# The queries' matrix of a decode kernel: one load of 64 KB pieces in place of two of 32 KB

## The chip, the cores and the metric

The kernel runs on one core of a Trainium2 chip. Its time is the device time of one execution, in microseconds. The core has five engines that run side by side and wait for each other by semaphores: TensorE (PE in the profile), VectorE (DVE), ScalarE (ACT), GpSimd (POOL) and SyncE (SP). Transfers between the chip's memory and the on-chip buffer of 128 partitions are issued by an engine's queue and carried out by 16 DMA engines. Before the change, three runs gave 684.35 us in the median (683.91 to 684.98).

## The reference, cut to what matters

One token x of 512 numbers is normalized; xn goes into attention over a cache of 8192 keys and values for each of 32 heads of width 128, and into a gated unit; the result is x + s * g, all in 32-bit floats.

```python
xn = _layernorm(x)                                   # 512
q = (xn @ wq).reshape(32 heads, 128)                 # wq: 512 x 4096, 8.39 MB
scores = einsum("hd,hkd->hk", q, k_cache) * 128**-0.5   # k_cache: 32 x 8192 x 128, 134 MB
p = softmax(scores)
o = einsum("hk,hkd->hd", p, v_cache)                 # v_cache: 134 MB
s = o.reshape(4096) @ wo                             # wo: 4096 x 512, 8.39 MB
g = silu((sigmoid(xn @ w_gate) * (xn @ w_up)) @ w_down)   # three of 2.82 MB
out = x + s * g
```

Each weight and each cached number is used once, so 293.67 MB are read for one token.

## The kernel before, in words

The work goes through three large buffers (`slots`) of 64 KB on each of the 128 partitions. Slots 0 and 1 hold keys in turn, slot 2 holds values. A load of keys or values covers one pair of heads: 2 x 8192 rows of 128 numbers, 8.39 MB, which fills a slot with one piece of 64 KB on each partition. There are 16 pairs.

Nearly all loads are issued by SyncE, in program order, on one queue (q1 in the profile). SyncE waits in front of a load until the slot is free, and every load behind it in the program waits with it. The order is: the queries' matrix, w_gate and w_up (both in slot 0), keys of pair 0 (slot 1), w_down (slot 2, when the queries are made), keys of pair 1 (slot 0, when TensorE has summed the gate's rows), values of pair 0 (slot 2, when the gated unit is done), and then in turn the keys of pair i (when the scores of pair i-2 are done with the slot, `summed[i - 2]`) and the values of pair i-1 (when TensorE is done with the values before, `valued`). At the end the last keys and values are cut into parts, and wo comes in seven loads. All loads pass through `load` (line 168) or `load_values` (line 227).

The queries' matrix `wq` lies in slot 2 until w_down and the values need it. Partition p holds rows 4p to 4p+3 of the matrix, one after the other; so the four blocks `wq_t[:, k, :]` of 4096 numbers lie side by side on each partition, and x is turned so that `xn[:, k]` fits them. Two loads bring blocks 0 and 1, then blocks 2 and 3: 32 KB on each partition each. The first load is issued ahead of `tc.close()` and `tc.compile()`, the second behind them. ScalarE issues the two small loads of x on its own queue (q10), which the same 16 DMA engines serve.

VectorE makes the queries' products in place. When x has landed it is turned (L261) and normalized in a chain of short steps with TensorE and ScalarE (L262 to L280). Then VectorE multiplies block 0 by `xn[:, 0]` (L290), and adds blocks 1 and 2 to it (L291), 4096 numbers wide; block 3 follows in eight stretches of 512 (L308). After each stretch TensorE sums the 128 partitions by a product with ones, into a PSUM bank, and ScalarE copies the sums to `q_all` (L312). So every partition has all queries that it needs.

w_gate and w_up are taken in the same way (L290 and L291, 1376 wide), summed by TensorE, made into the hidden row (L348 to L362) and multiplied by w_down. Then VectorE turns to the pairs: for each it multiplies the keys by the queries in place (L416), and sums each row (L417), which frees the keys' slot. TensorE, ScalarE and VectorE make the softmax without its division (L409, L429, L431), and TensorE multiplies the values (64 products of 512 columns) while VectorE is at the next pair's keys. The tail divides, places the result (L466 to L476) and multiplies by wo (L521, L523).

The profile's line L38 is the helper through which all of TensorE's instructions pass.

Of the kernel before, what the change touches and what calls it, by code (L numbers as in the profile page):

```python
# [51 lines left out]
def kernel(  # L52
# [16 lines left out]
    KT = D // P  # L69
# [23 lines left out]
    W_DVE = [r for r in range(W_FOLD) if r not in [r for r, _ in W_PE]]  # L93
    V_CUT, K_CUTS = NB // 2, {NP - 2: (NB * 3 // 4,), NP - 1: (NB * 23 // 32,)}

    N_SEMS = 36
    DVE, ACT, SP, POOL = nc.vector, nc.scalar, nc.sync, nc.gpsimd
    PE = Later(nc.tensor)
    pe_only = OrderedEngineSet([nc.tensor.engine])
# [2 lines left out]

    sems = [nc.alloc_semaphore(f"s_{i}") for i in range(N_SEMS)]
    s_out = nc.alloc_semaphore("s_out")
# [42 lines left out]
    def semaphore(name):  # L147
        return unused.pop(0)
# [14 lines left out]
    def load(eng, name, dst, src, *after):  # L163
        wait(eng, *after)
        if name not in loads:
            loads[name] = [semaphore(f"s_{name}"), 0]
        loads[name][1] += 16
        ins = eng.dma_start(dst, src)  # L168
        if not tc.compiled:
            tc.no_tile_sem_insts.add(ins.ins.name)  # L170
        ins.then_inc(loads[name][0], 16)
        return loads[name][0], loads[name][1]

    def wait(eng, *steps):
        for s in steps:
            if s is not None:
                eng.wait_ge(*s)
# [9 lines left out]

    xv = x.rearrange("a b d -> (a b d)")
    wq_t = slots[2].rearrange("p (k c) -> p k c", k=KT)
    wq_v = wq.rearrange("(p k) c -> p k c", k=KT)  # L190
    def load_queries(n):
        return load(SP, f"wq{n}", wq_t[:, n:n + 2, :], wq_v[:, n:n + 2, :])

    ld_wq = [load_queries(0)]
    tc.close()
    tc.compile()
    ld_wq.append(load_queries(2))
    wg_t, wu_t = (slots[0][:, n * KT * F:(n + 1) * KT * F].rearrange("p (k f) -> p k f", f=F) for n in range(2))
    ld_g = load(SP, "wg", wg_t, w_gate.rearrange("(p k) f -> p k f", k=KT))
    ld_u = load(SP, "wu", wu_t, w_up.rearrange("(p k) f -> p k f", k=KT))  # L200
# [61 lines left out]
    t = dve(DVE.reduce_sum(st[:, 0:1], x_col, axis=AX.X))  # L262
    wait(PE, t)
    t = pe(PE.matmul(pt[:, 0:1], ones, st[:, 0:1], start=True, stop=True))
    wait(DVE, t)
    t = dve(DVE.tensor_scalar(st[:, 1:2], pt[:, 0:1], 1.0 / D, None, op0=ALU.mult))
    wait(DVE, t)
    t = dve(DVE.tensor_scalar(xc, x_col, st[:, 1:2], None, op0=ALU.subtract))
    wait(DVE, t)
    t = dve(DVE.tensor_mul(sq, xc, xc))  # L270
    wait(DVE, t)
    t = dve(DVE.reduce_sum(st[:, 2:3], sq, axis=AX.X))
    wait(PE, t)
    t = pe(PE.matmul(pm[:, 0:1], ones, st[:, 2:3], start=True, stop=True))
    wait(ACT, t)
    t = act(ACT.activation(st[:, 3:4], pm[:, 0:1], AF.Sqrt, bias=eps_t, scale=1.0 / D))
    wait(DVE, t)
    t = dve(DVE.reciprocal(st[:, 4:5], st[:, 3:4]))
# [8 lines left out]
    def in_place(w, k, cols=slice(None)):  # L287
        y = w[:, 0, cols]
        if k == 0:
            return dve(DVE.tensor_scalar(y, y, xn[:, 0:1], None, op0=ALU.mult))  # L290
        return dve(DVE.scalar_tensor_tensor(y, w[:, k, cols], xn[:, k:k + 1], y, op0=ALU.mult, op1=ALU.add))  # L291
# [1 line left out]

    wait(DVE, c_xn)
    for k in range(KT - 1):
        wait(DVE, ld_wq[k // 2] if k % 2 == 0 else None, t if k else None)
        t = in_place(wq_t, k)
    wait(DVE, t)
    before_q = PE.take()
# [5 lines left out]
    for t in range(NQ):  # L305
        c = slice(t * QT, (t + 1) * QT)
# [29 lines left out]
    for dst, src, ld in zip(sums, (wg_t, wu_t), (ld_g, ld_u)):  # L336
        wait(DVE, ld)
        for k in range(KT):
            t = in_place(src, k)
# [7 lines left out]
    for d, c in zip(sums[0], chunks):  # L347
        t = act(ACT.activation(sg[:, c], d[:, :c.stop - c.start], AF.Sigmoid))  # L348
    wait(DVE, t, rows[1])
    for d, c in zip(sums[1], chunks):  # L350
        t = dve(DVE.tensor_mul(hg[:, c], sg[:, c], d[:, :c.stop - c.start]))
# [6 lines left out]
    n = FL // NG  # L358
    for g in range(NG):
        r = slice(g * GP, (g + 1) * GP)  # L360
        h = hg[r, NG * FW + g * n:NG * FW + (g + 1) * n].rearrange("p (i c) -> p c i", c=FC)
        t = dve(DVE.transpose(hid[r, FP:, :].rearrange("p c (i m) -> p c i m", m=NG),  # L362
                              h.unsqueeze(3).to_broadcast([GP, FC, n // FC, NG])))
# [128 lines left out]
    def copies(g):  # L492
        return GP if g % 2 == 0 else 1
# [21 lines left out]
    for k, r in enumerate(W_DVE):  # L515
        n = k % 2
# [21 lines left out]
    for r in direct:  # L538
        landed(PE, r, direct)
        for g in range(NG):  # L540
            n = copies(g)
# [6 lines left out]
    t = dve(DVE.tensor_mul(g_row, g_row, acc))  # L548
# [66 lines left out]
```

## Time and profile before

| what | value |
|---|---|
| median of three runs | 684.35 us (683.91 to 684.98) |
| the profiled execution | 683.9 us |
| its span, first to last instruction | 682.5 us |
| read from memory | 293.67 MB, 430 GB/s over the span |
| SyncE's queue q1 | 6968 packets, 99.5% of 16 DMA engines' span |
| VectorE | 613.4 us busy, 90% of the span |
| TensorE | 220.8 us busy, 32% of the span, mean granted clock 0.670 |
| the two loads of the queries' matrix | 4096 KB each, 16.3 us from issue to landing in the median |

Times in rows of the profile are microseconds from the start of the span, unless marked ns. A row of the timeline has the start, the duration, the engine (a trailing q marks its queue, where DMAs are issued), the line, the operation, what is written and read, the shapes, the count, and in brackets how long the engine had been idle and what ended that. A row of a stretch has its bounds and length, the busy time of each engine with the count of its instructions, TensorE's granted clock, the mean busy share of the 16 DMA engines, and GB/s; a packet counts in the stretch in which it starts, so short stretches swing. A row of a queue has packets, MB and the time of its packets as a share of the 16 engines' time.

### The profile page before, as it was taken

The page shows a single profiled execution, that of the slowest core. Times are in us where ns is not written, and L with a number is a line of the kernel's source. Part 1 is how long each engine was busy: PE and PEld are TensorE (multiplying, and loading weights), DVE is VectorE, ACT ScalarE, POOL GpSimd, SP SyncE. Part 2 cuts the span into 40 slices and gives each one's busy share as a digit, 9 for nine tenths or more (in the row PEclk, how much of TensorE's full clock was granted, in tenths as well). Part 3 has the DMA queues.
Part 4 walks back from the last instruction along what each step waited for, and adds up shares of the span by engine and source line. Part 5 has one row for each costly group of instructions (what it writes and reads, how often), then busy time and mean ns, then how long its engine had stood idle before and what let it go on. Part 6 is the DMA issues. An engine that isn't in the chain of part 4 may idle for free. (4 is left out here: it accounts for less than half of the span.)

```text
span 682.5 us, 3396 instructions
## 1 busy us (share of the span) xinstructions
PE 220.8 (32%) x1386; PEld 63.9 (9%) x1386; DVE 613.4 (90%) x151; ACT 44.6 (7%) x142; POOL 2.6 (0%) x11
## 2 busy tenths in 40 slices
PE   0353024060513305060512306050412406053368
PEld 0120001010100101010100101010100101011111
DVE  2979999999999998998979899898989899999926
ACT  2130010000000100000000100000010100000010
POOL 0000000000000000000000000000000000000000
PEclk9985658575665758575665758575665858575869
DMA  9999999999999999999999999999999999999998
GB/s 380 430 442 461 442 430 430 430 430 430 430 430 430 430 430 430 438 446 446 453 430 430 430 430 430 430 430 430 430 430 430 430 447 422 475 422 409 436 428 341
DMA packets 6988, 293.68 MB, mean 430 GB/s; under 512 B 798, under 2 KB 812, under 8 KB 1228
## 3 DMA queue, kind: packets, MB, share of 16 engines
q1 hardware_dynamic: 6968, 293.67, 99.5%
q10 hardware_dynamic: 20, 0.01, 0.0%
HBM read 293.67 MB, written 0.00 MB: 430 GB/s over the span
## 5 line engine op out<-in xcount | busy, mean ns | idle before, releaser
L416 DVE TENSOR_TENSOR slot<-slot,q_all 128x16384 f32<-128x16384 f32 (+4 forms) x18 | 275.8, 15323 | 23.6 <-DMA slot<-in_A_k_cache_dram 23.6
L417 DVE TENSOR_REDUCE sc<-slot 128x128 f32<-128x16384 f32 (+4 forms) x18 | 275.8, 15324 | 0.6
L38 PE MATMUL psum<-slot,zeros 128*8 128x512 f32 x1028 | 148.4, 735 | 251.6 <-PEq L38 251.6
L38 PEld LDWEIGHTS psum<-slot,zeros 128*8 128x8 f32 x1028 | 30.7, 103 | 354.9 <-issue 354.9
L38 PE MATMUL psum<-ident,mx 128*1 128x128 f32 x32 | 9.2, 387 | 117.6 <-PEq L38 117.6
L438 ACT COPY o<-psum 128x512 f32<-128x512 f32 x16 | 9.4, 586 | 396.2 <-PE psum L38 396.2
L38 PE MATMUL psum<-slot,ones 128*128 (+3 forms) x36 | 15.8, 614 | 19.2 <-PEq L38 13.8
L38 PE MATMUL psum<-o,pick 128*2 128x128 f32 x128 | 16.5, 272 | 12.8 <-PEq L38 12.8
L291 DVE SCALAR_TENSOR_TENSOR slot<-slot,xn 128x1376 f32<-128x1376 f32 (+1 forms) x8 | 18.9, 2360 | 0.7 <-DMA slot<-in_A_wq_dram 0.4
L424 DVE STREAM_TRANSPOSE psum<-psum 32x128 f32<-32x128 f32 x16 | 4.9, 309 | 9.9 <-PE psum L38 9.9
L429 ACT ACTIVATE nb<-psum 128x2 f32<-128x2 f32 x16 | 2.8, 172 | 160.9 <-PE psum L38 160.9
L38 PEld LDWEIGHTS psum<-ident,mx 128*1 128x1 f32 x32 | 1.8, 80 | 121.8 <-issue 121.8
L431 ACT ACTIVATE zeros<-sc,nb 64x128 f32<-64x128 f32 x32 | 12.8, 400 | 0.9
L38 PEld LDWEIGHTS psum<-o,pick 128*2 128x2 f32 x128 | 9.9, 84 | 29.6 <-issue 27.2
L409 DVE TENSOR_REDUCE mx<-psum 1x2 f32<-1x128 f32 x16 | 4.5, 279 | 8.5 <-PE psum L38 8.5
L38 PE MATMUL psum<-slot,o_all 128*1 128x512 f32 (+2 forms) x60 | 11.3, 423 | 1.1 <-DMA slot<-in_A_wo_dram 1.1
L38 PE MATMUL psum<-zeros,rs 128*32 128x2 f32 x32 | 3.8, 189 | 23.6 <-PEq L38 23.6
L38 PE MATMUL psum<-mx,ones 1*128 1x2 f32 x32 | 8.8, 343 | 7.4 <-PEq L38 7.4
L38 PE MATMUL psum<-slot,o 128*1 128x512 f32 x26 | 5.9, 976 | 13.2 <-DMA slot<-in_B_w_down_dram 13.2
L38 PEld LDWEIGHTS psum<-mx,ones 1*128 1x128 f32 x32 | 7.9, 305 | 14.7 <-issue 14.7
L38 PEld LDWEIGHTS psum<-slot,ones 128*128 128x128 f32 (+1 forms) x36 | 6.3, 203 | 28.4 <-issue 20.7
L261 DVE STREAM_TRANSPOSE g_row<-x_row 128x128 f32<-128x128 f32 x1 | 0.4, 402 | 9.3 <-DMA x_row<-in_A_x_dram 9.3
(54 smaller groups left out, 69.6 us busy)
## 6 DMA issues: line engine op xcount, KB each, us to landing
slot<-in_A_v_cache_dram SPq DMA_DIRECT2D x4, 4096.0 KB, 19.3
slot<-in_A_wq_dram SPq DMA_DIRECT2D x2, 4096.0 KB, 16.3
slot<-in_A_k_cache_dram SPq DMA_DIRECT2D x1, 6144.0 KB, 37.9
slot<-in_A_k_cache_dram SPq DMA_DIRECT2D x1, 5888.0 KB, 37.4
slot<-in_A_wo_dram SPq DMA_DIRECT2D x1, 3072.0 KB, 26.2
slot<-in_B_w_gate_dram SPq DMA_DIRECT2D x1, 2752.0 KB, 26.7
slot<-in_B_w_up_dram SPq DMA_DIRECT2D x1, 2752.0 KB, 32.7
slot<-in_B_w_down_dram SPq DMA_DIRECT2D x1, 2560.0 KB, 23.6
```

The source lines that it names most:

```text
L38: ins = getattr(self.engine, name)(*args, **kwargs)
L261: wait(DVE, dve(DVE.transpose(x_turned, x_row.rearrange("p (i k) -> p k i", k=KT))))
L291: return dve(DVE.scalar_tensor_tensor(y, w[:, k, cols], xn[:, k:k + 1], y, op0=ALU.mult, op1=ALU.add))
L409: DVE.reduce_max(mx[:1, 1:3], pt[0:1, :].rearrange("o (e p) -> o e p", e=2), axis=AX.X).then_inc(reduced, 1)
L416: wait(DVE, dve(DVE.tensor_mul(k[:, j, :], k[:, j, :], qb[:, i:i + 1, :].to_broadcast([P, n, Dh]))))
L417: summed[i] = dve(DVE.reduce_sum(sc[i % 2][:, j], k[:, j, :], axis=AX.X))
L424: turned_out[i] = dve(DVE.transpose(o, pn.rearrange("e (a r) -> e a r", r=WR)))
L429: wait(ACT, act(ACT.mul(nb, pm[:, :2], -SCALE)))
L431: ACT.activation(weights[h, :, e * HT:(e + 1) * HT], sc[i % 2][h].rearrange("p (g b) -> p g b", b=HT), AF.Exp, bias=nb[h, e:e + 1], scale= ...
L438: ACT.copy(o1, po).then_inc(copied, 1)
```

## The change

The two loads of the queries' matrix become one, issued where the first was. Each of its pieces is 64 KB on a partition, where the two loads had 32 KB each. VectorE waits for the whole load ahead of block 0, where it waited for the first half ahead of block 0 and for the second ahead of block 2. One semaphore less is needed. Nothing else is changed.

```diff
-    N_SEMS = 36
+    N_SEMS = 35
...
     wq_t = slots[2].rearrange("p (k c) -> p k c", k=KT)
-    wq_v = wq.rearrange("(p k) c -> p k c", k=KT)
-    def load_queries(n):
-        return load(SP, f"wq{n}", wq_t[:, n:n + 2, :], wq_v[:, n:n + 2, :])
-
-    ld_wq = [load_queries(0)]
+    ld_wq = load(SP, "wq", wq_t, wq.rearrange("(p k) c -> p k c", k=KT))
     tc.close()
     tc.compile()
-    ld_wq.append(load_queries(2))
...
     wait(DVE, c_xn)
     for k in range(KT - 1):
-        wait(DVE, ld_wq[k // 2] if k % 2 == 0 else None, t if k else None)
+        wait(DVE, t if k else ld_wq)
         t = in_place(wq_t, k)
```

## The prediction

> **What bounds the kernel now.** I read the page's head, its DMA part and its share per line first, because a kernel that reads 293.67 MB and computes little is likely to hang on its transfers.
>
> ```profile
> span 682.5 us, 3396 instructions
> PE 220.8 (32%) x1386; PEld 63.9 (9%) x1386; DVE 613.4 (90%) x151; ACT 44.6 (7%) x142; POOL 2.6 (0%) x11
> q1 hardware_dynamic: 6968, 293.67, 99.5%
> HBM read 293.67 MB, written 0.00 MB: 430 GB/s over the span
> L416 DVE TENSOR_TENSOR slot<-slot,q_all 128x16384 f32<-128x16384 f32 (+4 forms) x18 | 275.8, 15323 | 23.6 <-DMA slot<-in_A_k_cache_dram 23.6
> ```
>
> SyncE's queue q1 fills the 16 DMA engines for 99.5% of the span. VectorE is 90% busy and waits 23.6 us for keys. Two resources are nearly full, so I cut the span into stretches and asked for the DMA share of each, then looked where VectorE's first wait for keys stands.
>
> ```profile
> 1.50:1.76 0.26, 0.00 (x0) 0.00 (x0) 0.00 (x0) 0.00 (x0) 0.00 (x0) 1.00 0.00 0
> 1.75:12.05 10.30, 0.00 (x0) 0.00 (x0) 0.55 (x2) 3.34 (x6) 0.97 (x6) 1.00 1.00 408
> 12.05:21.72 9.67, 1.17 (x4) 1.00 (x4) 7.77 (x10) 0.26 (x1) 0.00 (x0) 1.00 1.00 434
> 20.00:99.20 79.20, 23.12 (x68) 8.04 (x68) 73.15 (x36) 12.05 (x29) 1.38 (x1) 0.71 1.00 431
> 97.50:99.20 1.70, 0.00 (x0) 0.00 (x0) 1.70 (x1) 0.00 (x0) 0.00 (x0) 0.50 0.00 0
> 99.20:99.80 0.60, 0.00 (x0) 0.00 (x0) 0.60 (x1) 0.00 (x0) 0.00 (x0) 0.50 4.04 1748
> 99.20:640.00 540.80, 169.19 (x1148) 47.97 (x1152) 508.98 (x75) 26.46 (x98) 0.00 (x0) 0.64 1.00 434
> ```
>
> The last two columns are the share and the GB/s of packets that start in the stretch. The first packet starts at 1.76; from there to 640 us the share is 1.00 in every long stretch. The stream has no hole. (A short stretch shows 0.00 when all engines are inside one long packet: that is how 97.5 to 99.2 reads, and it tells that all 16 engines finish their last piece of the first values at 99.2 to 99.8.) So the end of the kernel is the end of one unbroken stream, and an edit costs time only where it makes that stream run dry, or changes its rate.
>
> Next, the timeline of the prologue and of the first two head pairs: who issues loads, and when.
>
> ```profile
> 0.74 1.54 SPq L168 DMA_DIRECT2D slot<-in_A_wq_dram  x2
> 2.40 1.67 ACTq L168 DMA_DIRECT2D x_row<-in_A_x_dram  x2
> 11.67 0.40 DVE L261 STREAM_TRANSPOSE g_row<-x_row 128x128 f32<-128x128 f32 x1 [9.30 <-DMA x_row<-in_A_x_dram]
> 15.19 2.35 DVE L290 TENSOR_SCALAR slot<-slot,xn 128x4096 f32<-128x4096 f32 x1
> 17.58 4.49 DVE L291 SCALAR_TENSOR_TENSOR slot<-slot,xn 128x4096 f32<-128x4096 f32 x1
> 22.50 4.48 DVE L291 SCALAR_TENSOR_TENSOR slot<-slot,xn 128x4096 f32<-128x4096 f32 x1 [0.43 <-DMA slot<-in_A_wq_dram]
> 37.27 1.98 SPq L168 DMA_DIRECT2D slot<-in_B_w_down_dram  x2
> 38.37 2.58 PE L38 MATMUL psum<-slot,ones 128*128 128x512 f32 x6 [1.13 <-DVE slot L291]
> 44.53 3.81 PE L38 MATMUL psum<-slot,ones 128*128 128x512 f32 x6 [3.59 <-DVE slot L291]
> 48.38 0.33 SPq L168 DMA_DIRECT2D slot<-in_A_k_cache_dram  x1
> 55.44 17.23 DVE L416 TENSOR_TENSOR slot<-slot,q_all 128x16384 f32<-128x16384 f32 x1
> 68.60 0.33 SPq L227 DMA_DIRECT2D slot<-in_A_v_cache_dram  x1
> 89.95 0.33 SPq L168 DMA_DIRECT2D slot<-in_A_k_cache_dram  x1
> 91.22 17.20 DVE L416 TENSOR_TENSOR slot<-slot,q_all 128x16384 f32<-128x16384 f32 x1
> 100.14 8.82 PE L38 MATMUL psum<-slot,zeros 128*8 128x512 f32 x64 [5.24 <-PEq L38]
> 109.02 0.33 SPq L227 DMA_DIRECT2D slot<-in_A_v_cache_dram  x1
> 126.97 17.20 DVE L416 TENSOR_TENSOR slot<-slot,q_all 128x16384 f32<-128x16384 f32 x1
> 235.30 17.23 DVE L416 TENSOR_TENSOR slot<-slot,q_all 128x16384 f32<-128x16384 f32 x1 [0.99 <-DMA slot<-in_A_k_cache_dram]
> ```
>
> VectorE starts on the queries at 15.19, when x is normalized and the first half of the matrix has come; it needs the second half at 22.07 and gets it at 22.50. Its chain then runs without a wait for a transfer to 235.30. In this stretch the loads' issues hang on VectorE: the third keys go out at 89.95, when the first scores are done with their slot. There the change can reach the stream.
>
> **The change, part by part.** (1) *One issue fewer on SyncE, one semaphore and one set of completion packets fewer.* SyncE's issues at the start are 45 us ahead of what the stream works on, and the stream shows no hole at the border of the two loads (share 1.00 from 12.05 on, the border being there). Cost 0, gain 0. Without the cover of a full queue a saved issue would be worth at most 1.54/2 = 0.8 us.
>
> The Trainium skill (DMA: Bandwidth & Descriptors, "Anatomy of one DMA") gives each DMA a fixed cost of about 2.0 us, by its words mostly the receipt at the end. By that, one load fewer would save 2.0 us; the share of 1.00 across the border speaks against it.
>
> (2) *Pieces of 64 KB instead of 32 KB.* The keys and values have that size already: between 62 and 96 us the DMA part counts 240 packets with 14.68 MB, 16 of them completions, so 65.5 KB each, at the 99.6% below.
>
> ```profile
> q1 hardware_dynamic: 240, 14.68, 99.6%
> ```
>
> Rate 431 GB/s (20 to 99) or 434 (later) against 434 for the second half of the matrix: the same. Cost 0; the first stretch (408 GB/s) shows what an empty queue costs at its start, 10.3 x 26/434 = 0.6 us, and I expect it unchanged.
>
> (3) *The first multiplication waits for all of the matrix.* The bytes ahead of it are the same, so it all lands at 22.5. VectorE does 22.07 - 15.19 = 6.9 us of work before it needs the second half; that work now begins at 22.5 instead of ending there. So everything behind it on VectorE is D = 22.5 + 6.9 - 22.5 = 6.9 us later, if xn is there by 22.5.
>
> (4) *x comes later.* ScalarE issues x's two small loads at 2.40, behind nothing of its own, but they share the 16 engines. I counted packets by queue in short stretches: 2.40 to 7.10, then 7.10 to 7.70, 8.35 to 8.85, 9.58 to 10.06 and 10.8 to 11.3.
>
> ```profile
> q1 hardware_dynamic: 49, 1.61, 80.2%
> q10 hardware_dynamic: 4, 0.00, 1.1%
> q10 hardware_dynamic: 4, 0.00, 0.5%
> q10 hardware_dynamic: 2, 0.00, 0.7%
> q10 hardware_dynamic: 2, 0.00, 0.2%
> ```
>
> After the issue 49/16 = 3 pieces per engine (100 KB) of the matrix start before x's queue q10 gets its first turn at 7.1; then it gets one turn after each further piece: data, completion, data, completion, 1.2 us apart (32 KB x 16 / 434 GB/s = 1.21). With 64 KB pieces the three gaps between turns take 3 x 2.41 instead of 3 x 1.21, so x is 3.6 us later at least, at 15.3. The first turn comes at the same 7.1 if what is ahead counts in bytes, and after four pieces from the start, at 7.1 + 4 x 1.21 = 12.0, if it counts in pieces: x at 20.1. From L261 to L290 x takes 15.19 - 11.67 = 3.5 us more, so xn is ready at 18.8 to 23.6. Another place tells which: at the end ScalarE stores x_row at 664.49, and 84 packets, 16 of them completions, start before its first packet (664.49 to 667.95).
>
> ```profile
> q1 hardware_dynamic: 84, 1.44, 97.1%
> ```
>
> That is 4.25 pieces and 90 KB per engine, against 3.1 and 100 KB above: the bytes agree better. I take bytes, xn at 18.8, hidden by the matrix itself (22.5); by pieces D is 6.9 + 1.1 = 8.0.
>
> (5) *What D moves.* Loads behind VectorE go out D later. The stream needs each when all before it is read: w_down at the end of the first keys (8.39 MB of query matrix, 2 x 2.82 of w_gate and w_up, 8.39 of keys: 22.41 MB, of which 4.19 by 12.05), 12.05 + (22.41 - 4.19)/0.435 = 54, issued 37.3 + 6.9 = 44.2; second keys at 60.4, issued 55.3; first values at 79.7, issued by 75.5; all early. The third keys are needed at 99.2 and go out at 89.95 + 6.9 = 96.9. From issue to first packet an idle queue takes 1.76 - 0.74 = 1.0, so they are ready at 97.9: 1.3 us early. Cost 0. This is the thin place: the cover there shrinks from 8.2 us (99.2 - 89.95 - 1.0) to 1.3. The second values wait for TensorE's 64 matmuls, which start at 100.14 on landing; powers would now come about 1.5 us after that, and the issue moves to 111 (at most 116 if TensorE's clock is halved throughout), needed at 99.5 + 8.39/0.434 = 118.8.
>
> TensorE's clock can move D itself: the same six matmuls took 2.58 at the clock before and 3.81 partly behind its drop, so between 2.58 and 2 x 2.58 = 5.16: -1.2 to +1.35 on all that follows them.
>
> (6) *D dies out.* A pair costs VectorE 126.97 - 91.22 = 35.75 and the stream 2 x 8.39 MB/434 GB/s = 38.7. VectorE gains 2.9 per pair; its first wait for keys moves from 235.3 about three pairs later, to 351, and the 23.6 us of waiting shrink to 16.7. At the end nothing is left of it.
>
> **Sum.** 0 + 0 + 0 on the stream: the profiled execution, 683.9 us (span 682.5), stays 683.9; the median of the runs shown is 684.35, 0.45 above it. I forecast 684.4.
>
> **Rivals.**
> *A. The third keys come late (slower).* One mechanism, at 99.2 us: each microsecond of D over 8.2 empties the stream for one, plus 0.6 for starting an empty queue. With x counted in pieces (8.0) and TensorE slow (+1.35) D is 9.35: 1.15 + 0.6 = 1.75 us, 686.1. For it: the cover of 1.3; against: both must come together.
> *B. x waits for the whole matrix (slower).* x's first turn only after all of the load, at 21.7, then three turns behind pieces of w_gate (2.75 MB, 22 KB pieces, 0.81 us each): x at 21.7 + 2.4 + 0.5 = 24.6, xn 28.1, D = 6.9 + 5.6 = 12.5, the stream dry for 4.3 + 0.6: 689.3. Against it: x had its turn after 64 of the first half's 128 pieces, and after single pieces from there.
> The Trainium skill (the same page, "Queues, rings and completion order") says that an engine drains a whole packet, typically 9 to 17 descriptors, from one queue before it turns to the next. With a load's 8 pieces per engine as one packet that would be B; the alternation above disagrees.
> *C. The delay is carried to the end (slower).* 684.35 + 6.9 = 691.3. Against: the waits for keys from 235.3 on, 23.6 us in all, absorb it.
> *D. A load fewer is a fixed cost fewer (faster).* A hole at the border as long as the start's latency and slow rate, 1.0 + 0.6 = 1.6: 682.8. Against: share 1.00 there.
> *E. The pieces stay 32 KB (no change in kind).* x stays at 11.6, D stays 6.9, 684.4. Against: the 65.5 KB pieces of the keys.
>
> **How the numbers follow.** A difference under 0.2% (1.4 us) can't be told from none in this kernel. Forecast 0.82 and E 0.02 give no change, 684.4; A beyond 0.2%: 0.08; B 0.03; C 0.02; D 0.03. Faster 0.03, same 0.84, slower 0.13. The range reaches from 683.6, the runs' own spread below, to 686.1, A's price; B, C and D stay outside.
>
> **What would show it.** Right: the share stays 1.00 from 1.8 to 640; L261 at about 15 to 20; L290 waits for in_A_wq at 22.5; the first L416 at about 62, the issue now at 89.95 at about 97; the first wait for keys near 351, 16.7 us in all. Step 4 is wrong if L261 stays near 11.7 or passes 20.5, step 5 if packets of the third keys start after 99.8. The forecast is wrong if the stream has a hole, or if the span changes without one.

## The result, and the profile after

The changed kernel takes 685.88 us in the median of 22 runs (684.23 to 687.12), the kernel before 684.35 us (683.88 to 685.79, 22 runs). The ratio is 1.0019 with a 95% interval of 1.0013 to 1.0025: 1.3 us slower by the ratio, 1.5 us by the medians. The first is just inside the 0.2% (1.4 us) which the prediction called no change, the second just outside. The time is inside the prediction's range of 683.6 to 686.1, but with this many runs the interval excludes a ratio of 1. The profiled execution after took 685.87 us, with a span of 684.5 us: 2.0 us more than before.

The lines of the page after that answer to those of before; the long rows are the 40 slices of the span.

```profile
span 684.5 us, 3394 instructions
DMA  9999989999999999999999999999999999999997
GB/s 383 425 441 467 433 368 433 440 452 440 433 433 433 429 429 429 429 429 429 429 437 467 437 429 437 429 429 429 429 429 429 429 440 430 470 416 427 421 434 332
q1 hardware_dynamic: 6824, 293.67, 99.3%
L411 DVE TENSOR_TENSOR slot<-slot,q_all 128x16384 f32<-128x16384 f32 (+4 forms) x18 | 275.7, 15318 | 17.0 <-DMA slot<-in_A_k_cache_dram 16.9
```

The bytes are the same. The sixth slice, 86 to 103 us, moves 368 GB/s where the slices on either side move 433, and its DMA share is 8 tenths: the stream that had no hole before has one now. VectorE waits less for keys (16.9 us against 23.6), so it lost its slack there and not at the end.

The stretches around that slice, in the columns of the prediction's stretches (the last two are the DMA share and GB/s):

```profile
97.60:99.20 1.60, 0.00 (x0) 0.00 (x0) 1.57 (x2) 0.00 (x0) 0.00 (x0) 0.50 0.00 0
99.20:99.90 0.70, 0.42 (x2) 0.11 (x2) 0.13 (x1) 0.00 (x0) 0.00 (x0) 0.50 0.01 0
99.90:101.00 1.10, 0.64 (x3) 0.50 (x2) 0.90 (x2) 0.00 (x0) 0.00 (x0) 0.50 2.73 953
103.00:640.00 537.00, 169.13 (x1138) 47.92 (x1142) 512.01 (x75) 27.19 (x103) 0.00 (x0) 0.64 1.00 433
```

Before, all 16 engines went over from the first values to the third keys between 99.2 and 99.8. After, no piece starts there; 953 GB/s x 1.1 us = 1.05 MB = 16 pieces start between 99.9 and 101.0. They are slower too: the share times the length of the stretch gives 4.04 x 0.60 = 2.42 us for each of the 16 pieces before, and 2.73 x 1.10 = 3.00 us for each of the 16 after the hole. From 103 us on the share is 1.00 again.

The timeline after, with the rows on which the lateness can be followed:

```profile
15.12 0.40 DVE L256 STREAM_TRANSPOSE g_row<-x_row 128x128 f32<-128x128 f32 x1 [12.76 <-DMA x_row<-in_A_x_dram]
22.83 2.35 DVE L285 TENSOR_SCALAR slot<-slot,xn 128x4096 f32<-128x4096 f32 x1 [4.22 <-DMA slot<-in_A_wq_dram]
35.45 9.75 PE L38 MATMUL psum<-slot,ones 128*128 x16 [17.60 <-PEq L38]
45.26 1.38 POOL L319 MEMSET slot<- 128x1536 f32 x1 [41.96 <-PE psum L38]
45.59 1.78 DVE L285 TENSOR_SCALAR slot<-slot,xn 128x1376 f32<-128x1376 f32 x1
52.49 4.95 PE L38 MATMUL psum<-slot,ones 128*128 128x512 f32 x6 [3.82 <-DVE slot L286]
57.47 0.33 SPq L168 DMA_DIRECT2D slot<-in_A_k_cache_dram  x1
64.53 17.23 DVE L411 TENSOR_TENSOR slot<-slot,q_all 128x16384 f32<-128x16384 f32 x1
99.04 0.33 SPq L168 DMA_DIRECT2D slot<-in_A_k_cache_dram  x1
353.20 17.23 DVE L411 TENSOR_TENSOR slot<-slot,q_all 128x16384 f32<-128x16384 f32 x1 [2.55 <-DMA slot<-in_A_k_cache_dram]
```

The third keys go out at 99.04, where they went out at 89.95: 9.1 us later, and less than a microsecond ahead of the moment at which the engines run out of work. The line numbers are lower by five because the change shortens the file (L261 is now L256, L290 is L285, L416 is L411).

### The profile page after: what moved, and what is told of

It reads as the page before. It is cut to its first block, busy times and chain, and to the rows that moved or that the text cites. A ratio compares the mean times of both kernels' runs of the same rounds, so it can differ in the third digit from the quotient of the medians.

```text
span 684.5 us, 3394 instructions
## 1 busy us (share of the span) xinstructions
PE 223.7 (33%) x1386; PEld 64.9 (9%) x1386; DVE 613.8 (90%) x151; ACT 44.6 (7%) x142; POOL 2.6 (0%) x11
## 3 DMA queue, kind: packets, MB, share of 16 engines
q1 hardware_dynamic: 6824, 293.67, 99.3%
## 5 line engine op out<-in xcount | busy, mean ns | idle before, releaser
L411 DVE TENSOR_TENSOR slot<-slot,q_all 128x16384 f32<-128x16384 f32 (+4 forms) x18 | 275.7, 15318 | 17.0 <-DMA slot<-in_A_k_cache_dram 16.9
L38 PE MATMUL psum<-slot,zeros 128*8 128x512 f32 x1028 | 150.3, 743 | 208.2 <-PEq L38 208.2
L38 PE MATMUL psum<-slot,ones 128*128 (+3 forms) x36 | 17.7, 668 | 23.0 <-PEq L38 17.6
L256 DVE STREAM_TRANSPOSE g_row<-x_row 128x128 f32<-128x128 f32 x1 | 0.4, 402 | 12.8 <-DMA x_row<-in_A_x_dram 12.8
L38 PE MATMUL psum<-zeros,rs 128*32 128x2 f32 x32 | 3.8, 189 | 23.6 <-PEq L38 23.6
L285 DVE TENSOR_SCALAR slot<-slot,xn 128x1376 f32<-128x1376 f32 (+1 forms) x3 | 5.1, 1689 | 4.3 <-DMA slot<-in_A_wq_dram 4.2
```

Of the source, the lines that this page charges most:

```text
L38: ins = getattr(self.engine, name)(*args, **kwargs)
L256: wait(DVE, dve(DVE.transpose(x_turned, x_row.rearrange("p (i k) -> p k i", k=KT))))
L411: wait(DVE, dve(DVE.tensor_mul(k[:, j, :], k[:, j, :], qb[:, i:i + 1, :].to_broadcast([P, n, Dh]))))
```

## The experiments

The theory after this profile: VectorE's chain starts late, so the third keys go out late, so the stream runs dry near 100 us. The rivals: 64 KB pieces are slower in themselves; x that comes late is the cause; something else behind VectorE comes late; each load has a fixed cost.

### Two loads of 32 KB pieces, but a wait for both

```diff
-        wait(DVE, ld_wq[k // 2] if k % 2 == 0 else None, t if k else None)
+        wait(DVE, *([t] if k else ld_wq))
```

(against the kernel before)

> Two loads of 32 KB pieces as before the change, but VectorE waits for both of them ahead of block 0. Theory (the third keys go out late, because VectorE's chain starts late): x lands at about 11.7, L290 starts at 22.5, the third keys go out at 97 to 99.5 as in the changed kernel, and the time is 684.4 to 686.4, near 685.6, with a hole in the stream near 100 us of 0 to 1.7 us. Rival 1 (pieces of 64 KB are slower in themselves): no loss here, 684.4, whatever VectorE does. Rival 2 (x that comes late is the cause): no loss here either, since x lands early.

Measured: 685.52 us in the median (684.32 to 687.55, 11 runs), ratio 1.0016 (1.0007 to 1.0025). The timeline of its profile:

```profile
11.52 0.40 DVE L261 STREAM_TRANSPOSE g_row<-x_row 128x128 f32<-128x128 f32 x1 [9.15 <-DMA x_row<-in_A_x_dram]
22.63 2.35 DVE L290 TENSOR_SCALAR slot<-slot,xn 128x4096 f32<-128x4096 f32 x1 [7.63 <-DMA slot<-in_A_wq_dram]
98.57 0.33 SPq L168 DMA_DIRECT2D slot<-in_A_k_cache_dram  x1
```

A loss of the same size within the intervals (1.0016 against 1.0019) is there with the loads of before, with pieces of 32 KB, and with x at 11.5. So it needs neither the larger pieces nor a late x; the wait alone is enough.

### The changed kernel, with the third keys loaded early

```diff
+    EARLY, halfway = pieces(NB // 2), []
+    ld_k[0] = [(j, ld_k[0][0][1]) for j in EARLY]
...
             summed[i] = dve(DVE.reduce_sum(sc[i % 2][:, j], k[:, j, :], axis=AX.X))
+            halfway.append(summed[i])
...
-            load_keys(i, k_cut[:1] if i == NP - 1 else k_cut, summed[i - 2])
+            if i == 2:
+                load_keys(i, EARLY[:1], halfway[0])
+                load_keys(i, EARLY[1:], summed[0])
+            else:
+                load_keys(i, k_cut[:1] if i == NP - 1 else k_cut, summed[i - 2])
```

> The changed kernel, with the scores of the first pair made in two halves and the third keys loaded in two halves, the first as soon as its half of the slot is free: about 17 us before the 99 us of the changed kernel, so at about 82. Nothing else of the delay is taken away. Theory (late third keys): no hole near 100 us, 684.4 to 684.8, of which up to 0.2 us is the slower start of the stream with 64 KB pieces. Rival 1 (64 KB pieces): 685.9 as the changed kernel. Rival 2 (something else behind VectorE that comes late, as the second values): a hole elsewhere, near 119 us, and 685 to 686.

Measured: 684.30 us (683.99 to 685.04, 11 runs), ratio to the kernel before 0.9997 (0.9988 to 1.0006). Its timeline and stretches:

```profile
22.75 2.35 DVE L285 TENSOR_SCALAR slot<-slot,xn 128x4096 f32<-128x4096 f32 x1 [3.88 <-DMA slot<-in_A_wq_dram]
35.38 8.59 PE L38 MATMUL psum<-slot,ones 128*128 x16 [17.27 <-PEq L38]
51.57 4.27 PE L38 MATMUL psum<-slot,ones 128*128 128x512 f32 x6 [3.46 <-DVE slot L286]
80.37 17.65 SPq L168 DMA_DIRECT2D slot<-in_A_k_cache_dram  x2
```

```profile
99.20:640.00 540.80, 172.74 (x1152) 48.58 (x1156) 516.45 (x77) 29.02 (x105) 0.00 (x0) 0.64 1.00 434
```

The one load of 64 KB pieces and the wait for all of it are still there, and VectorE still starts at 22.75. Only the third keys have half of their slot at 80.4. The loss is gone and the share is 1.00 from 99.2 on. The profile alone would not show it: TensorE's sums were quick in it (8.59 and 4.27 us, against 9.75 and 4.95 in the profile after), so the second half already went out at about 97.7 (80.37 + 17.65 - 0.33), and a whole load at 97.50 cost nothing measurable either in a profile further down. The 11 runs do: none is above 685.04, where half of the changed kernel's 22 are above 685.88. This is the experiment that pins the cause: all that can be measured of the loss is the lateness of that one load.

### The kernel before, with idle work for VectorE

```diff
+    wait(DVE, dve(DVE.memset(q_all, 0.0)))
+    for n in range(5):
+        t = dve(DVE.reduce_sum(st[:, 5 + n:6 + n], q_all, axis=AX.X))
+    wait(DVE, t)
     for k in range(KT - 1):
```

> The kernel before, with about 12 us of idle work for VectorE ahead of block 0 (a fill of q_all and five sums over 2048 numbers, whose results are not used). Two loads of 32 KB pieces, waits as before. Theory: VectorE's chain is 11.8 us later, the third keys go out at about 101.7 (100.5 to 103.7 with TensorE's clock), the stream is dry for 101.7 + 1.0 - 99.5 = 3.2 us (2 to 5) and 0.6 us slow at its new start: 688.2 (687 to 690). A chain that is late for another reason than the queries' load costs the same. Rivals: 64 KB pieces or late x as the cause would give 684.4.

Measured: 690.73 us (689.29 to 692.51, 6 runs), ratio 1.0088 (1.0073 to 1.0103): above the range I had given. The profile shows what I had missed, a second hole ahead of the first:

```profile
28.59 2.35 DVE L290 TENSOR_SCALAR slot<-slot,xn 128x4096 f32<-128x4096 f32 x1
51.42 2.23 DVE L290 TENSOR_SCALAR slot<-slot,xn 128x1376 f32<-128x1376 f32 x1
51.54 1.38 POOL L328 MEMSET slot<- 128x1536 f32 x1 [48.24 <-PE psum L38]
63.75 0.33 SPq L168 DMA_DIRECT2D slot<-in_A_k_cache_dram  x1
```

```profile
61.30:64.70 3.40, 2.42 (x4) 0.67 (x2) 0.85 (x2) 0.00 (x0) 0.00 (x0) 0.50 0.00 0
104.70:106.20 1.50, 0.45 (x2) 0.11 (x2) 0.87 (x2) 0.00 (x0) 0.00 (x0) 0.50 0.00 0
```

VectorE started 13.4 us late instead of 11.8, and with 15.4 us of lateness at their issue (63.75 against 48.38) the second keys missed the end of w_down as well. Both holes stand at a place where the stream has run out of issued work; in the first, nothing of any size starts between 61.3 and 64.7. So a late chain costs time in a kernel whose queries' matrix comes in two loads, and the cost doesn't grow evenly: each load has its own cover.

### GpSimd's fill behind VectorE's multiplication

In the profile after, the first multiplication of w_up took 1.78 us (the row at 45.59), against 1.06 before, beside a fill by GpSimd.

```diff
-    wait(POOL, spread_all)
-    c_rest = pool(POOL.memset(wd_rest, 0.0))
-    ld_d = load(SP, "wd", wd_last[0:P:NG], ..., c_rest)
...
             t = in_place(src, k)
+            if rows and k == 0:
+                wait(POOL, spread_all, t)
+                c_rest = pool(POOL.memset(wd_rest, 0.0))
+                ld_d = load(SP, "wd", wd_last[0:P:NG], ..., c_rest)
             wait(DVE, t)
```

> The changed kernel, with GpSimd's fill of w_down's rest (1.38 us) moved behind VectorE's first multiplication of w_up, which in the changed kernel's profile ran 1.78 us beside that fill where it ran 1.06 before. Theory (the two hold each other up, and this is 0.7 us of the third keys' delay): that multiplication takes 0.7 to 0.9, the third keys go out 0.8 to 1.1 us earlier than in the changed kernel, near 98.1, and the time falls by about as much as the hole had, 0.6 to 1.1 us: near 685.0. Rival (the longer row has another reason, such as TensorE's clock): 1.78 stays or the time stays at 685.9.

Measured: 684.50 us (684.00 to 685.77, 11 runs), where near 685.0 was expected; ratio to the kernel before 1.0001 (0.9992 to 1.0010), with the one load still in it. Over these runs the loss is gone here too. SyncE's queue and a stretch in its profile:

```profile
97.50 0.33 SPq L168 DMA_DIRECT2D slot<-in_A_k_cache_dram  x1
```

```profile
99.20:99.90 0.70, 0.34 (x2) 0.25 (x2) 0.70 (x1) 0.31 (x2) 0.00 (x0) 0.50 3.27 1404
```

The third keys go out at 97.50, 1.5 us earlier than in the changed kernel's profile, and the hole is gone. But in that profile TensorE's 16 sums happened to take 8.54 us, so the fill would have been early anyway; it doesn't show which of the two moved the issue. So the same kernel was profiled again.

> A second profile of the kernel with GpSimd's fill behind VectorE's first multiplication of w_up. Theory: whatever TensorE's clock does to the 16 sums (8.5 to 10.2 us), that multiplication takes 0.7 to 1.0 us, never 1.5 to 2.2, because the fill is behind it; the third keys go out at 97.2 to 98.4. No hole if that is up to 97.7; a hole of 1 to 2.5 us is possible if it is nearer to 98.4. Rival (TensorE's clock lengthens the multiplication, not the fill): 1.5 to 2.2 again where the 16 sums take 9.5 or more.

The timeline of the second profile:

```profile
35.35 9.74 PE L38 MATMUL psum<-slot,ones 128*128 x16 [17.53 <-PEq L38]
45.49 0.94 DVE L285 TENSOR_SCALAR slot<-slot,xn 128x1376 f32<-128x1376 f32 x1
46.55 1.38 POOL L334 MEMSET slot<- 128x1536 f32 x1 [43.25 <-DVE slot L285]
51.54 4.95 PE L38 MATMUL psum<-slot,ones 128*128 128x512 f32 x6 [2.97 <-DVE slot L286]
98.09 0.33 SPq L168 DMA_DIRECT2D slot<-in_A_k_cache_dram  x1
```

Here TensorE's sums take 9.74 and 4.95, as in the profile after (9.75 and 4.95), and the multiplication takes 0.94 and not 1.78: the fill was what held it up, and 0.84 of the 0.95 us by which the issue is earlier come from it. All the same this execution took 687.13 us, more than the profile after and more than any of the 11 runs: 0.95 us earlier was not cheaper. That is the next point.

### Further profiles of the changed kernel and of the wait for both

Both kernels were profiled again, unaltered, to set the hole against the time of the issue.

> A second profile of the changed kernel, unaltered. Theory: TensorE's clock comes up at another moment, so the 16 sums of the queries take 8.5 to 10.2 us and the six sums of w_up 2.6 to 5.2; the third keys go out between 96.5 and 99.5 and the span follows: issue up to 97.7, span near 682.9 and no hole; issue near 99, span 684 to 685 and a hole near 100 us. Rival (the loss is in the pieces, not in the issue): the span stays near 684.5 whatever the issue.

> A third profile of the changed kernel, unaltered; expected as the second: the span follows the time at which the third keys go out, with no hole up to 97.7 and 1 to 2 us near 99.

> A second profile of the kernel with two loads of 32 KB pieces and a wait for both. The third keys go out between 96.5 and 99.3, by TensorE's clock. If the hole's price is a matter of how late the issue is alone, an issue at or before 98.57 costs no more than the 2.9 us of the first profile of this kernel, and one after it more; the profiles of the changed kernel (99.04: 1.4 us; 99.30: 1.8; 98.76: 2.4) speak against that, and for a price between 0 and 3 us whose size within a microsecond of the stream's end isn't set by the issue time.

| profile | third keys issued | their pieces started by 99.85, of 16 | third keys landed | span |
|---|---|---|---|---|
| before | 89.95 | 16 | 119.4 | 682.5 |
| fill later | 97.50 | 14 | 119.5 | 683.2 |
| wait for both, second | 98.81 | 5 | 120.8 | 684.0 |
| changed | 99.04 | 0 | 120.8 | 684.5 |
| changed, second | 99.30 | 0 | 121.2 | 684.8 |
| changed, third | 98.76 | 6 | 121.9 | 685.6 |
| fill later, second | 98.09 | 11 | 121.9 | 685.8 |
| wait for both | 98.57 | 4 | 122.7 | 686.2 |

(Pieces: the MB that queue q1 starts between 97.60 and 99.85, by 0.0655. Landed: the issue and the profile's time from issue to landing, 29.4 us before and 21.8 to 24.1 in the others. The rows are in order of the span.) At 97.50 no loss can be told: 683.2 lies within the spans of the kernel before in its other runs, 682.5 to 683.3. From 98.09 on there is one, but it does not grow with the issue: the three dearest profiles lie between 98.09 and 98.76, not at 99.30. I had expected a span near 682.9 for an early issue and a steady price after it; the first was not among these two profiles of the changed kernel, the second is wrong. The span goes with the landing instead, in all eight rows: none lands earlier than the one above it, and from first to last the landing moves by 3.3 us and the span by 3.7. What the dear ones share is a straggler. The stretch from 101 to 102 us, in the order fill later second, wait for both, changed third, and last the changed kernel's second profile:

```profile
101.00:102.00 1.00, 0.00 (x0) 0.00 (x0) 1.00 (x1) 0.99 (x3) 0.00 (x0) 0.50 0.58 197
```

```profile
101.00:102.00 1.00, 0.00 (x0) 0.00 (x0) 1.00 (x1) 1.00 (x1) 0.00 (x0) 0.50 0.39 131
```

```profile
101.00:102.00 1.00, 0.00 (x0) 0.00 (x0) 1.00 (x1) 0.98 (x2) 0.00 (x0) 0.50 0.21 66
```

```profile
101.00:102.00 1.00, 0.34 (x2) 0.26 (x2) 1.00 (x1) 0.60 (x2) 0.00 (x0) 0.50 0.00 0
```

In the three profiles above 685.5 us, three, two and one pieces (197, 131 and 66 GB/s x 1 us, by 0.0655 MB) start between 101 and 102 us, while most engines had theirs a microsecond or more before; in the others none does. So the price goes with the engines that get their first piece last, and a late landing is where it shows. Why single engines get it 2.2 us and more after the issue, when others have had theirs in about 1 us, no run here tells; it stays open.

### Four loads of 16 KB pieces

```diff
-        return load(SP, f"wq{n}", wq_t[:, n:n + 2, :], wq_v[:, n:n + 2, :])
+        return load(SP, f"wq{n}", wq_t[:, n:n + 1, :], wq_v[:, n:n + 1, :])
...
-    ld_wq.append(load_queries(2))
+    ld_wq += [load_queries(n) for n in range(1, KT)]
...
-        wait(DVE, ld_wq[k // 2] if k % 2 == 0 else None, t if k else None)
+        wait(DVE, ld_wq[k], t if k else None)
         t = in_place(wq_t, k)
-    wait(DVE, t)
+    wait(DVE, t, ld_wq[KT - 1])
```

> The queries' matrix in four loads, one block of 16 KB pieces each, with a wait ahead of each block. Theory (what costs is the lateness of the third keys, and the size of the first pieces only sets how slowly an empty queue starts): x's three gaps of turns shrink from 1.21 to 0.6 us each, so L261 starts at about 9.9 and L290 at 13.4; VectorE's chain is 1 to 2 us earlier than before the change, the third keys go out at 87 to 89; no hole; the time is 684.2 to 684.5, no different from before, since the stream was without holes already; the matrix has landed up to 0.1 us earlier. Rival (a load costs a fixed time on the stream): two more loads than before cost 2 to 4 us, 686.4 to 688.4, and a hole shows at each border.

Measured: 684.13 us (683.94 to 684.63, 11 runs), ratio 0.9993 (0.9984 to 1.0002).

```profile
9.31 0.40 DVE L261 STREAM_TRANSPOSE g_row<-x_row 128x128 f32<-128x128 f32 x1 [6.95 <-DMA x_row<-in_A_x_dram]
12.83 2.35 DVE L290 TENSOR_SCALAR slot<-slot,xn 128x4096 f32<-128x4096 f32 x1
54.96 17.23 DVE L416 TENSOR_TENSOR slot<-slot,q_all 128x16384 f32<-128x16384 f32 x1 [1.85 <-DMA slot<-in_A_k_cache_dram]
89.47 0.33 SPq L168 DMA_DIRECT2D slot<-in_A_k_cache_dram  x1
```

Two loads more than before cost nothing that can be measured, so a load has no fixed price on this stream, which always has work. VectorE starts 2.4 us earlier than before, and that buys nothing either, since the third keys were in time already. Their issue moves by 0.5 only (it was expected at 87 to 89), because VectorE now waits 1.85 us for the first keys, which land at 54.96.

## Why the prediction was right or wrong

The time lay in the range, and 684.4 was within 0.22% of 685.88. But the forecast said that the stream gets no hole, and it got one; by its own sign that makes the forecast wrong. What happened is the place and about the price of rival A, to which I gave 0.08 and for which the range was stretched to 686.1. So the number came out by the smallness of the price, which is luck, and not by the mechanism.

Steps 3 and 5 rest on these rows beside those shown above, the first two from before, the third from after:

```profile
27.02 5.39 DVE L308 SCALAR_TENSOR_TENSOR slot<-slot,xn 128x512 f32<-128x512 f32 x8
28.21 9.03 PE L38 MATMUL psum<-slot,ones 128*128 x16 [13.81 <-PEq L38]
34.26 5.39 DVE L303 SCALAR_TENSOR_TENSOR slot<-slot,xn 128x512 f32<-128x512 f32 x8
```

- **Step 1, one issue fewer, cost 0: right.** The run with four loads (0.9993) shows it from the other side. The fixed cost of about 2.0 us from the page "DMA: Bandwidth & Descriptors" of the Trainium skill, which the prediction set against this step, is not to be seen in either direction. (The section fits that cost to DMAs issued by GpSimd; SyncE issues these.)
- **Step 2, the pieces' rate: right, their start a little too cheap.** The whole matrix has landed at 22.83, 22.68 and 22.80 in the three profiles of the changed kernel, against 22.50 before and 22.63 and 22.68 with 32 KB pieces and the wait for both. The means are 22.77 and 22.60: 64 KB pieces at an empty queue may cost 0.2 us, not 0, but profiles with the same loads differ by as much, and the run with early keys (0.9997) says that it can't be told in the time.
- **Step 3, 6.9 us of order: right.** VectorE starts its last block at 34.26 (L303) against 27.02 (L308): 7.24, of which 0.33 is the matrix landing later (22.83 against 22.50).
- **Step 4, x: right.** L256 starts at 15.12; by bytes 15.3 was forecast, by pieces 20.1. Its queue's first turn comes at 7.3, where counting by bytes gave 7.1 and counting by pieces 12.0. Rival B, with x behind the whole matrix, falls with it; the Trainium skill's rule of whole packets (the same page, "Queues, rings and completion order"), read with a load's eight pieces per engine as one packet, doesn't describe these loads.
- **Step 5, the third keys ready 1.3 us early, cost 0: wrong.** Its own sign was packets that start after 99.8, and all 16 do. The failed step is the sum of D at that issue: 9.1 us, not 6.9. It is made of 6.91 of order, 0.33 of landing, and two terms that I had at 0: 0.72 us (1.78 against 1.06) by which GpSimd's fill holds up VectorE's first multiplication of w_up, and 1.14 us (4.95 against 3.81) by which TensorE's six sums of w_up run slower. The second I had bounded at +1.35, and then taken as 0; the first I had not seen, though the fill stood in the trace of before. It comes from TensorE too: the fill waits for the 16 sums of the queries, which took 9.75 us in place of 9.03, so it began 0.72 us later against VectorE's chain. Together 9.10, and 99.04 - 89.95 = 9.09. Rival A asked for 8.2 and got there without x being late. The other covers held as worked out: the second keys went out at 57.47, needed at 60.4.
- **The price in rival A: mis-sized.** By A, 9.1 - 8.2 + 0.6 = 1.5 us; the profile lost 2.0 in the span, and the runs 1.5 in the median. The 0.6 is there in the profile after, as pieces of 3.00 us in place of 2.42. But the rule (one for one, plus 0.6) doesn't hold from profile to profile: those of the same kernel, and of the ones beside it, lost 1.5 to 3.7 us for issues between 98.09 and 99.30, and the latest issue was not the dearest. What A left out is that the engines don't start together.
- **Step 6, D dies out: right.** The first wait for keys stands at 353.20 (351 forecast), and the waits add up to 16.9 us (16.7 forecast). The agreement is closer than it deserves: D was 2.2 us larger, and the stream 2 us later, and the two offset each other.
- **Rivals C, D and E fell:** 691.3 and 682.8 are far off. That the pieces are of 64 KB in fact is shown by the first row of x (15.12, not 11.6) and by the packets of q1: 6824 against 6968, which is 128 pieces and 16 completions fewer.

Why the changed kernel's runs spread over 2.9 us where the kernel before and the one with early keys keep within 1.9 and 1.05 is only partly shown: its issue stands on the edge, and TensorE's clock and the stragglers move it from run to run. That both do so is seen in the profiles; how much each gives to a run's time is not.

## What to carry to other kernels

In a kernel that is bound by one unbroken stream of loads, ask of every edit which later load's issue it delays, and how much cover that issue has; an edit that moves no bytes can still cost what exceeds the cover. A cover that shrinks to about a microsecond, as here, is gone: terms of a microsecond or less that cost nothing anywhere else (another engine's fill, a slower clock) add up on the same chain, so take their bad ends and not their middle. Where the cover is thin, split the work that frees the buffer and issue the load in two parts: here that alone took back the whole loss.

## What the runs showed of the hardware

**A fill by GpSimd stops a multiplication by VectorE.** Four more rows, from the changed kernel's second profile and from the kernel before, with those shown above:

```profile
45.44 2.19 DVE L285 TENSOR_SCALAR slot<-slot,xn 128x1376 f32<-128x1376 f32 x1
45.52 1.38 POOL L319 MEMSET slot<- 128x1536 f32 x1 [42.23 <-PE psum L38]
```

```profile
37.30 1.38 POOL L324 MEMSET slot<- 128x1536 f32 x1 [33.99 <-PE psum L38]
38.35 1.06 DVE L290 TENSOR_SCALAR slot<-slot,xn 128x1376 f32<-128x1376 f32 x1
```

Before, the fill ends at 38.68 and the multiplication at 39.41; after, 46.64 and 47.37; in the second profile, 46.90 and 47.63; with idle work, 52.92 and 53.65. The multiplication ends 0.73 us after the fill each time, however much they overlap, and takes 0.94 when nothing overlaps: it does not run slower beside the fill, it stands still until the fill is done. The Trainium skill (SBUF — State Buffer, "SBUF: two separate sides") says that VectorE, in some of its modes, and GpSimd share one pair of ports, which the one that starts first holds for its whole instruction while the other blocks. That the loser blocks entirely agrees with these rows. Whether the first to start wins can't be read from them: in the second profile VectorE's row starts 0.08 us ahead of the fill and is held up all the same, but 0.94 - 0.73 = 0.21 us of the multiplication pass before it is stopped, so its row may begin before it needs the ports.

**TensorE's clock depends on the moment.** The granted clock is the column ahead of the DMA share: for the six sums of w_up before, after, and in the first profile with the fill later:

```profile
44.53:48.34 3.81, 3.81 (x6) 1.35 (x6) 0.00 (x0) 0.00 (x0) 0.00 (x0) 0.66 1.11 482
```

```profile
52.49:57.44 4.95, 4.95 (x6) 1.84 (x6) 0.00 (x0) 0.00 (x0) 0.00 (x0) 0.50 0.71 306
```

```profile
51.63:55.90 4.27, 4.27 (x6) 1.64 (x6) 0.00 (x0) 0.00 (x0) 0.00 (x0) 0.60 1.00 433
```

The same six products take 3.81, 4.95 and 4.27 us at clocks of 0.66, 0.50 and 0.60; the 16 sums of the queries took from 8.54 to 10.19 us in the profiles. The Trainium skill (TensorE: Matmul & The Clock Gate, "What's actually happening") has the clock follow activity in windows of about 3.4 us that run freely and don't restart with a kernel; three executions of the changed kernel with 16 sums of 9.75, 10.16 and 9.49 us agree with that.

**A small load beside a large one waits for one piece a turn.** With pieces of 16, 32 and 64 KB ahead of it, x is there at 9.31, 11.67 and 15.12: it takes its turns between single pieces. In the packets of queue q10 its first turn comes at 6.7, 7.2 and 7.3 us, nearly the same whatever the pieces, and the turns after it are 0.6, 1.2 and 2.4 us apart.
